# Sliding-window attention and a multiplicative feed-forward on one core: gates on GpSimd, parted up products, half loads and a last tile in column halves

## The chip, the cores and the metric

The kernel runs on one NeuronCore of a Trainium2 chip. The metric is the device time of one execution in microseconds (us). A core has TensorE (PE, matrix products into PSUM), VectorE (DVE), ScalarE (ACT), GpSimd (POOL) and SyncE (SP), each with a queue of its own that it works off in order, and 16 DMA engines. PSUM has eight banks; each matrix product of this kernel is written to one bank, a group of scores to four and a value step to two.

## The reference

```python
# q, k, v: (8 batches, 8 heads, 576 rows, 64); heads 0-3: plain window of 32; heads 4-7: 32 rows at a distance of 4
scores = q @ k.T / 8;  scores = where(mask[h], scores, -1e9)
attn = exp(scores - max) / (sum + 1e-9)
x = (attn @ v) as (4608 tokens, 512)
out = ((x @ w1) * (x @ w2)) @ w3 @ w_out        # 512 -> 1024 -> 1024 -> 512, float32 out
```

## The kernel before

**Data flow.** q, k and v come in row form. VectorE transposes 32 x 32 blocks (`turn`, lines 379 and 394) so that the head dimension lies on partitions. The queries stand in an order by residue modulo 4, so that the dilated window is a plain window of 32 in each residue class. A half batch `u` (0: plain heads, 1: dilated heads) has six blocks `m` of 96 queries against 128 keys. `Group.scores` (line 445) writes scores of up to five blocks over four banks; `exps` (line 456, ScalarE) takes the exponential into a tile `et`; in later batches `masks` (line 464, VectorE) multiplies by a 0/1 mask, which GpSimd makes once in `masks_of_bias` (line 358), while batch 0 has a bias added by matmuls (line 428). A `Step` covers three blocks of one half: `values` (line 481) multiplies by v with a column of ones, `recip` and `norm` (lines 492, 504, VectorE) divide, and `back` and `keep` (lines 521, 529) transpose on TensorE and copy into XT in the first two batches; later batches use a DMA transpose. So each batch has four steps, 0 to 3. Batch 0 and 1 bring v through transposes on TensorE (`v_back`, line 403) and copies (`v_keep`, lines 413 and 415).

**The feed-forward** works in 16 units of 288 tokens. For a unit k and an f of eight 128-column slices, `up` (line 553) makes A(k,f) with w1 and B(k,f) with w2, each four matmuls over the four 128-row chunks of x, in the order 2, 3, 0, 1. Chunks 0 and 1 come from the plain heads (steps 0 and 1 of the batch), chunks 2 and 3 from the dilated heads (step 2 for an even unit, step 3 for an odd one). `copy_a` (line 564) takes A to SBUF as bf16 on ScalarE; `gate` (line 569) multiplies it by B, straight from PSUM, on VectorE, into `gt`. `down` (line 580) multiplies a tile of 128 tokens by the fused weight, 8 matmuls of 512 columns; `copy_y` (line 591) takes it to SBUF and `store` writes it out. The fused weight wf = w3 @ w_out is made once: `w3_back` (line 622) transposes a slice of w3, `w3_keep` (line 629) copies it on ScalarE, `w3_mul` (line 634) multiplies, and `w3_done` (lines 645, 647) keeps the result. `finish` (lines 601, 602) ends the last tile.

**The planner.** Every piece of work is a task with an engine, a duration in ns, the tasks that it needs and a priority; the smaller number goes first. `Plan.run` plays them through in time: a free engine takes the ready task of best priority, and the order of starts is the order in which instructions are written to each engine's queue. The queue "DMA" of the plan is GpSimd: loads are issued from it, and identity, bias and masks are computed on it. A load occupies it for its issue time alone:

```python
if e == "DMA":
    free[e] = now + t.dur[0]
    if t.dur[1]:
        dma = max(dma, now + t.dur[0]) + t.dur[1]
        t.end = dma + 1900
```

Loads get a rising priority number in the order in which they are named: four for batch 0, then those of `FIRST_LOADS` ("w0" are two loads, columns of w1 and w2; "30" is slice 0 of w3; "o0" half of w_out; "q1" the q of batch 1), then those of later batches. The masks have 26.5, the gates -1. `RANK` and `FIRST` hold priorities of the kinds of attention work: T a transpose on VectorE, S scores, E exponential, VT and VK the two parts of bringing v, V values, N the division, X and K the way back into XT, W and C the w3 transposes and their copies. `ON_DVE` names the copies that VectorE does instead of ScalarE. As long as TensorE has nothing and the first up product has not begun, the plan adds fillers (`fill`, line 676); `warm_up` (line 659) stands at the beginning.

Of the kernel before, what the change touches and what calls it, by code (L numbers as in the profile page):

```python
# [19 lines left out]
S = 576  # L20
# [6 lines left out]
UNIT = 288  # L27
RING = 1152
BIG = 30000.0
BIASED = 1  # L30
LATE = False
TURNED = 2
DIRECT_V = 2
ORDER = (2, 3, 0, 1)
RES = (0, 2, 1, 3)
RANK = dict(E=0.4, VK=2, K=0.3, N=1.5, T=3, VT=0.3, S=0.4, V=0.05, X=0.2, W=6, C=-1)
FIRST = {"E": 2, "VK": 0.4, "K": 0.5, "N": 0.2, "T": 2, "VT": 0.05, "S": 0.2, "V": 0.05, "X": 0.4}
WARM = 14
FILL = 110
FIRST_LOADS = ("30", "31", "w0", "w1", "32", "w2", "o0", "o1", "q1", "k1", "33", "34", "v1", "35", "36", "37")  # L40
SHIFT = {}
ON_DVE = ("VK0.0.1", "VK1.0.1", "W3D1", "W3D3", "W3D7")
GRP = 5
WHOLE = ("qn", "kn")
BUSY = 4500
LEAD = 1.1


class Task:
# [10 lines left out]
class Plan:  # L60
# [119 lines left out]
def kernel(  # L180
# [46 lines left out]
    kts = [const.tile([P, 2, PADK + S, 2], BF16, name=f"kt{i}") for i in range(2)]  # L227
    qts = [const.tile([P, 2, S, 2], BF16, name=f"qt{i}") for i in range(2)]
    vts = [const.tile([P, 2, PADK + S, 2], BF16, name=f"vt{i}") for i in range(1)]
    warm = const.tile([P, 512], BF16, name="warm")  # L230

    def bank(n, dtype=F32):
        at = ps[:, plan.now.place or 0, :]
        return (at if dtype == F32 else at.bitcast(dtype))[:, 0:n]
# [79 lines left out]
    w3n, w3T = {}, {}  # L314
# [226 lines left out]
    held = {}  # L541
# [5 lines left out]
            return XT[0][:, b * BLK : (b + 1) * BLK, c, 48 * hf : 48 * hf + 48]  # L547
        return XT[1][:, k, c - 2, :].rearrange("p (r m t) -> p m r t", r=2, m=BLK)

    def up(k, f, w_sb, key):  # L550
        o = bank(UNIT)
        for j, c in enumerate(ORDER):
            nc.tensor.matmul(  # L553
                out=o,
                lhsT=w_sb[:, c, f * P : (f + 1) * P],
                rhs=unit_cols(k, c),
                start=(j == 0),
                stop=(j == DCH - 1),
            )
        held[(key, k, f)] = o  # L560

    def copy_a(k, f):
        a_sb = wk_pool.tile([P, UNIT], BF16, tag="asb", bufs=6, name="asb")
        nc.scalar.copy(out=a_sb, in_=held[("a", k, f)])  # L564
        held[("s", k, f)] = a_sb

    def gate(k, f):
        c0 = (k * UNIT) % RING
        nc.vector.tensor_tensor(  # L569
            out=gt[:, f, c0 : c0 + UNIT].rearrange("p (r m t) -> p m r t", r=2, m=BLK),  # L570
            in0=held[("b", k, f)].rearrange("p (m r t) -> p m r t", r=2, m=BLK),
            in1=held[("s", k, f)].rearrange("p (m r t) -> p m r t", r=2, m=BLK),
            op=AL.mult,
        )

    def down(i):
        y = bank(d_model)
        c0 = (i * P) % RING
        for f in range(KFF):
            nc.tensor.matmul(  # L580
                out=y,
                lhsT=gt[:, f, c0 : c0 + P],
                rhs=wf_sb[:, f, :],
                start=(f == 0),
                stop=(f == KFF - 1),
            )
        held[("y", i)] = y
# [3 lines left out]
        nc.scalar.copy(out=o_sb, in_=held[("y", i)])  # L591
        held[("o", i)] = o_sb

    def finish(i):

        o_sb = wk_pool.tile([P, d_model], F32, tag="osb", bufs=3, name="osb")
        b, x = i * P // S, i * P % S
        row = b * S + 4 * (x % RUN) + RES[x // RUN]
        rows = out[row : row + 4 * (P - 1) + 1 : 4, :]
        lo, hi = slice(0, d_model // 2), slice(d_model // 2, d_model)  # L600
        nc.scalar.copy(out=o_sb[:, lo], in_=held[("y", i)][:, lo])
        nc.vector.tensor_copy(out=o_sb[:, hi], in_=held[("y", i)][:, hi])
        nc.scalar.dma_start(out=rows[:, lo], in_=o_sb[:, lo])
        nc.sync.dma_start(out=rows[:, hi], in_=o_sb[:, hi])

    def store(i):
        o_sb = held[("o", i)]
# [17 lines left out]
        held[("x3", ft)] = x  # L625

    def w3_keep(ft):
        w3T[ft] = wk_pool.tile([P, KFF, P], BF16, tag="w3T", bufs=3, name="w3T")
        nc.scalar.copy(out=w3T[ft], in_=held[("x3", ft)])  # L629

    def w3_mul(ft):
# [22 lines left out]
        return (RANK if b else FIRST)[kind]  # L654

    def warm_up():
        o = bank(512)
        for i in range(WARM):
            nc.tensor.matmul(out=o, lhsT=warm[:, 0:P], rhs=warm, start=True, stop=True)

# [12 lines left out]
            nc.vector.memset(t[0:32, :, 0, 0:D], 0.0)  # L673

    def fill():
        nc.tensor.matmul(out=bank(256), lhsT=warm[:, 0:P], rhs=warm[:, 0:256], start=True, stop=True)  # L676
# [18 lines left out]
    def loads_rows(nm, b, us=None):  # L695
        old = turned.get((nm, b - 2), [])
        for u in (0, 1) if us is None else us:
            L[(nm, b, u)] = None
        sl = slice(0, 2) if us is None else slice(us[0], us[-1] + 1)
        t = load(f"L{nm}{b}", 700, 3100 if us is None else 1600, old,  # L700
                 lambda: load_rows(nm, rows_of[nm], b, sl))
        for u in (0, 1) if us is None else us:
            L[(nm, b, u)] = t
# [26 lines left out]
    for u in range(2):  # L730
        for nm in ("qn", "kn", "vn"):
            if u or nm not in WHOLE:
                loads_rows(nm, 0, (u,))
# [6 lines left out]
    for x in FIRST_LOADS:  # L740
        c = int(x[1])
        if x[0] == "w":
            lw12[c] = loads_w12(c)
        elif x[0] == "o":
            lwo[c] = load(f"LWO{c}", 600, 3300, [], lambda c=c: load_wo(c))
        elif x[0] == "3":
            lw3[c] = load(f"LW3.{c}", 550, 1400, [], lambda ft=c: load_w3(ft))
        elif x[0] == "v" and DIRECT_V <= c:
            loads_v(c)
        else:  # L750
            loads_rows(x[0] + "n", c)

    FUSED, w3m = [], []
    for ft in sorted(lw3):
        x = add(f"W3T{ft}", "PE", 450, [lw3[ft], idt], lambda f=ft: w3_back(f), RANK["W"], slot=1,
                after=w3m[-3:-2])
        y = add("W3C", "ACT", 1012, [x], lambda f=ft: w3_keep(f), RANK["C"], lat=100, after=w3m[-3:-2])
        if ft + 7 in lw3:
            lw3[ft + 7].after.append(x)
            lw3[ft + 7].deps.append(x)  # L760
        z = add(f"W3M{ft}", "PE", 1728, [y, lwo[0], lwo[1]], lambda f=ft: w3_mul(f), 7, slot=1)
        w3m.append(z)
        name = f"W3D{ft}"
        eng, dur = ("DVE", 688) if name in ON_DVE else ("ACT", 585)
        FUSED.append(add(name, eng, dur, [z], lambda f=ft, e=eng: w3_done(f, e), -1, lat=100))
# [138 lines left out]
            prev["x"][i] = x  # L904
            vdone.setdefault(bb, []).append(vv)

    seq = 10
    G, Y, gates, stores, pairs = {}, {}, [], [], []

    def ups(k, f):  # L910
        nonlocal seq
        b, hf = k // 2, k % 2
        need = kept[b][0:2] + kept[b][2 + hf : 3 + hf]
        wl = lw12[(0, 0, 1, 1, 2, 2, 2, 2)[f]]
        lap = k * UNIT - RING
        free = [Y[i] for i in range(max(0, lap // P), (lap + UNIT - 1) // P + 1)]
        seq += 1
        a = add(f"A{k}.{f}", "PE", 490, need + wl, lambda: up(k, f, w1_sb, "a"), seq, slot=1,
                after=free + pairs[-1:])
        pairs.append(a)  # L920
        ca = add("CA", "ACT", 400, [a], lambda: copy_a(k, f), -1, lat=100,
                 after=[gates[-6] if len(gates) > 5 else None])
        seq += 1
        bb = add(f"B{k}.{f}", "PE", 490, need + wl, lambda: up(k, f, w2_sb, "b"), seq,
                 slot=1, after=[a])
        G[(k, f)] = add("G", "DVE", 460, [bb, ca], lambda: gate(k, f), -1, lat=100)
        gates.append(G[(k, f)])

    def downs(i):
        nonlocal seq  # L930
        seq += 1
        ks = {i * P // UNIT, (i * P + P - 1) // UNIT}
        y = add(f"Y{i}", "PE", 1728, [G[(k, f)] for k in ks for f in range(KFF)] + FUSED,
                lambda: down(i), seq, slot=1)
        Y[i] = y
        if i == n_y - 1:
            add("FIN", "ACT", 400, [y], lambda: finish(i), -1, lat=100, after=stores[-3:-2])
            return
# [58 lines left out]
```

## Time and profile before

| | |
|---|---|
| median of 3 runs | 256.36 us (256.32 to 256.38) |
| profiled execution, own time | 256.45 us |
| its span | 254.7 us |
| granted TensorE clock | 0.999 |
| first up product on TensorE | 21.6 us |
| first fused-weight product | 36.0 us |
| last matmul ends | 250.4 us |
| 128 gates on VectorE (line 569) | 57.7 us, 455 ns each |
| 128 copies of A on ScalarE (line 564) | 50.8 us, 398 ns each |
| five mask instructions on GpSimd (line 358) | 4.76 us together |

The time is that of the whole execution; the span is from the first instruction to the last, and 1.75 us lie around it. In timelines the columns are start in us, length in us, engine, line, operation with output and inputs, count, and in brackets the idle time before it with what ended it.

### The profile page before, as it was taken

To read this page: it belongs to the slowest core of one execution; us is meant where nothing else is said; L and a number is where in the kernel's file an instruction comes from. 1 tells how busy PE (TensorE), PEld (TensorE's weight loads), DVE (VectorE), ACT (ScalarE), POOL (GpSimd) and SP (SyncE) were. 2 spreads that over 40 slices of the span, in tenths; PEclk is the share of its full clock that TensorE was granted. 3 is DMA by queue.
4 is the path that set the end of the run, shared out by engine and by line. 5 is a ranking of instruction groups with operands and counts; after the bars stand their busy time and mean duration, and the time that the engine had idled before them with its cause. 6 is when DMAs were issued, how large, how long until landed. Compare 5 with 4: busy or idle time off the path is not lost.

```text
span 254.7 us, 6758 instructions
## 1 busy us (share of the span) xinstructions
PE 244.5 (96%) x2723; PEld 169.2 (66%) x2755; DVE 165.4 (65%) x341; ACT 126.0 (49%) x221; POOL 66.3 (26%) x103
## 2 busy tenths in 40 slices
PE   7699999999999999999999999999999999999993
PEld 3488766565767666667676766676767667777661
DVE  3983447799889888678767877837737365333220
ACT  5677333986635534462626526355353543333331
POOL 7653129543522712008260310700000000000000
PEclk9999999999999999999999999999999999999999
DMA  7999999999999999828999967952232223311113
GB/s 224 210 198 206 205 212 210 208 100 190 188 136 168 210 181 181 190 66 143 165 118 136 141 76 103 133 88 64 66 65 67 66 68 67 106 41 44 41 41 124
DMA packets 59230, 33.40 MB, mean 131 GB/s; under 512 B 44736, under 2 KB 49088, under 8 KB 59200
## 3 DMA queue, kind: packets, MB, share of 16 engines
q0 software_dynamic: 38544, 18.81, 58.6%
q1 hardware_dynamic: 20512, 14.03, 23.4%
q8 instruction: 21, 0.34, 0.6%
q10 hardware_dynamic: 144, 0.13, 0.2%
q14 instruction: 9, 0.07, 0.1%
HBM read 38.80 MB, written 9.44 MB: 189 GB/s over the span
## 4 chain that ended last, share of the span: by engine, by line
PE 92%; ACT 3%; DMA 2%; DVE 1%; issue 1%; ACTq 0%
PE ps L553 50%; PE ps L580 24%; PE ps L634 5%; PE ps L481 4%; PE ps L445 4%; DMA gt<-in_q_dram 2%; ACT et L456 2%; PE ps L676 2%; PE ps L622 1%; PE ps L403 1%; PE ps L521 1%; ACT w3T L629 1%; DVE qt L394 1%; ACT qn L271 0%; DVE kt L379 0%
## 5 line engine op out<-in xcount | busy, mean ns | idle before, releaser
L553 PE MATMUL ps<-XT,w_sb 128*128 128x288 bf16 x1024 | 136.2, 286 | 0.0
L553 PEld LDWEIGHTS <-w_sb 128*128 128x128 bf16 x1024 | 97.8, 98 | 30.6
L569 DVE TENSOR_TENSOR gt<-ps,asb 128x288 bf16<-128x288 f32 x128 | 57.7, 455 | 51.9 <-PE ps L553 49.6
L564 ACT CAST asb<-ps 128x288 bf16<-128x288 f32 x128 | 50.8, 398 | 51.9 <-PE ps L553 49.6
L580 PE MATMUL ps<-wf_sb,gt 128*128 128x512 bf16 x260 | 65.9, 379 | 1.5
L591 ACT COPY osb<-ps 128x512 f32<-128x512 f32 x35 | 20.5, 585 | 56.4 <-PE ps L580 54.6
L580 PEld LDWEIGHTS <-gt 128*128 128x128 bf16 x288 | 28.2, 98 | 27.8
L293 POOL DMA_DIRECT2D vp<-in_v_dram x48 | 29.9, 629 | 40.1 <-PE ps L481 20.8
L456 ACT ACTIVATE et<-ps 128x1920 bf16<-128x1920 f32 (+2 forms) x21 | 34.2, 1633 | 5.6 <-PE ps L445 4.8
L504 DVE TENSOR_TENSOR xo<-ps,rcp 96x384 bf16<-96x384 f32 (+1 forms) x48 | 31.5, 676 | 0.6
L464 DVE TENSOR_TENSOR et<-et,mask 128x960 bf16<-128x960 bf16 (+1 forms) x34 | 21.4, 646 | 4.9 <-ACT et L456 4.7
L394 DVE STREAM_TRANSPOSE qt<-qn 128x320 uint32<-128x320 uint32 (+3 forms) x34 | 22.4, 669 | 2.1 <-ACT qn L271 1.9
L481 PEld LDWEIGHTS <-et 128*128 128x128 bf16 x384 | 14.3, 98 | 1.7
L481 PE MATMUL ps<-vp,et 128*128 128x65 bf16 x384 | 15.1, 193 | 0.0
L634 PE MATMUL ps<-wo_sb,w3T 128*128 128x512 bf16 x60 | 14.4, 379 | 0.4
L394 DVE STREAM_TRANSPOSE kt<-kn 128x320 uint32<-128x320 uint32 (+3 forms) x18 | 11.6, 645 | 4.4 <-PE ps L445 4.3
L445 PE MATMUL ps<-qt,kt 32*128 32x96 bf16 x768 | 12.1, 201 | 1.9 <-DVE kt L379 1.9
L445 PEld LDWEIGHTS <-kt 32*128 32x128 bf16 x768 | 9.1, 92 | 7.0 <-issue 4.5
L492 DVE RECIPROCAL rcp<-ps 96x12 f32<-96x12 f32 x32 | 6.8, 216 | 10.5 <-PE ps L481 10.2
L245 POOL DMA_DIRECT2D kn<-in_k_dram x8 | 5.5, 685 | 29.0 <-DVE kt L394 16.7
L379 DVE STREAM_TRANSPOSE kt<-kn 128x576 uint32<-128x576 uint32 (+1 forms) x9 | 9.9, 1118 | 1.4 <-PE ps L445 1.4
L634 PEld LDWEIGHTS <-w3T 128*128 128x128 bf16 x64 | 5.9, 98 | 6.8 <-ACT w3T L629 0.6
(53 smaller groups left out, 114.6 us busy)
## 6 DMA issues: line engine op xcount, KB each, us to landing
qn<-in_q_dram POOLq DMA_DIRECT2D x7, 576.0 KB, 8.3
kn<-in_k_dram POOLq DMA_DIRECT2D x7, 576.0 KB, 7.5
w3n<-in_moe_w_dram POOLq DMA_DIRECT2D x8, 256.0 KB, 15.1
out_dram<-osb SPq DMA_DIRECT2D x7, 256.0 KB, 2.6
out_dram<-osb SPq DMA_DIRECT2D x8, 224.0 KB, 2.9
vp<-in_v_dram POOLq DMA_DIRECT2D x6, 288.0 KB, 10.4
out_dram<-osb SPq DMA_DIRECT2D x8, 192.0 KB, 2.7
out_dram<-osb SPq DMA_DIRECT2D x8, 160.0 KB, 3.9
```

What stands on the lines that cost most here:

```text
L293: nc.gpsimd.dma_start(out=vp[32 + p0 : 32 + p0 + n, 4:8, m, 0:D], in_=v_rows(b, 4, 4 * t0 + res, [[4 * D, n], [S * D, 4], [1, D]]),)
L394: nc.vector.transpose(out=o, in_=i)
L445: nc.tensor.matmul(out=self.sp[:, g, QB * i : QB * i + QB], lhsT=kt[prt, u, QB * m : QB * m + P, c], rhs=qq, start=(c == 0 and not biased) ...
L456: nc.scalar.activation(out=ev, in_=self.sp[:, :, 0:x], func=ACT.Exp, scale=scale)
L464: nc.vector.tensor_tensor(out=ev, in0=ev, in1=mk, op=AL.mult)
L481: nc.tensor.matmul(out=self.o[:, g, mm, :], lhsT=grp.et[:, c0 : c0 + P], rhs=vps[self.b % 2][:, 4 * self.u + g, 3 * self.hf + mm, 0 : D + ...
L504: nc.vector.tensor_tensor(out=dst, in0=self.o[0:QB, hs, :, 0:D], in1=self.rcp[0:QB, hs, :].unsqueeze(3).to_broadcast([QB, n, 3, D]), op=AL ...
L553: nc.tensor.matmul(out=o, lhsT=w_sb[:, c, f * P : (f + 1) * P], rhs=unit_cols(k, c), start=(j == 0), stop=(j == DCH - 1),)
L564: nc.scalar.copy(out=a_sb, in_=held[("a", k, f)])
L569: nc.vector.tensor_tensor(out=gt[:, f, c0 : c0 + UNIT].rearrange("p (r m t) -> p m r t", r=2, m=BLK), in0=held[("b", k, f)].rearrange("p ( ...
L580: nc.tensor.matmul(out=y, lhsT=gt[:, f, c0 : c0 + P], rhs=wf_sb[:, f, :], start=(f == 0), stop=(f == KFF - 1),)
L634: nc.tensor.matmul(out=o, lhsT=w3T[ft][:, g, :], rhs=wo_sb[:, g, :], start=(g == 0), stop=(g == KFF - 1),)
```

## The change

- `LATE` is set: the scores of batch 0's last step and the last v transposes wait for the values of step 2. Priorities, `LEAD` and the up products' first number differ. Warm-up is 24 matmuls of 256 columns instead of 14 of 512.
- Batch 1's loads come by halves ("k10" is k of batch 1, half 0), and in another order among the weights. `B0_LOADS` writes out batch 0's loads, in the order that they had.
- Twelve copies instead of five are on VectorE, K0.2 among them.
- Eighteen gates of units 0, 1 and 2 go to GpSimd: ScalarE first copies B to SBUF as float32 (`copy_b`), and GpSimd multiplies. There are two buffers for these copies.
- The first four up products are cut in two tasks: chunks 0 and 1, which need steps 0 and 1 alone, and then chunks 2 and 3.
- There are two buffers w3T instead of three.
- The last tile is made in two halves of 256 columns. VectorE copies the first, and 128 columns of the second; ScalarE copies the rest.

```diff
-LATE = False
+LATE = True
-RANK = dict(E=0.4, VK=2, K=0.3, N=1.5, T=3, VT=0.3, S=0.4, V=0.05, X=0.2, W=6, C=-1)
-FIRST = {"E": 2, "VK": 0.4, "K": 0.5, "N": 0.2, "T": 2, "VT": 0.05, "S": 0.2, "V": 0.05, "X": 0.4}
-WARM = 14
+RANK = dict(E=0.3, VK=0.2, K=1.5, N=0.4, T=0.2, VT=0.1, S=0.05, V=0.05, X=0.2, W=6, C=2)
+FIRST = {"E": 0.5, "VK": 2, "K": 0.5, "N": 1, "T": 1.5, "VT": 0.3, "S": 0.1, "V": 0.2, "X": 0.4}
+WARM = 24
-FIRST_LOADS = ("30", "31", "w0", "w1", "32", "w2", "o0", "o1", "q1", "k1", "33", "34", "v1", "35", "36", "37")
+FIRST_LOADS = ("w0", "30", "w1", "31", "k10", "w2", "o0", "o1", "32", "33", "q10", "v10", "v11", "34", "35", "36", "q11", "k11", "37")
-ON_DVE = ("VK0.0.1", "VK1.0.1", "W3D1", "W3D3", "W3D7")
+ON_DVE = ("K0.2", "K1.1", "K1.2", "VK0.0.0", "VK0.0.1", "VK0.1.1", "VK1.0.0", "W3D0", "W3D2", "W3D4", "W3D5", "W3D6")
+B0_LOADS = ("v0", "q1", "k1", "v1")
+ON_POOL = ("G0.0", "G0.2", "G0.3", "G0.4", "G0.6", "G0.7", "G1.0", "G1.1", "G1.2", "G1.4", "G1.6", "G1.7", "G2.1", "G2.2", "G2.3", "G2.4", "G2.5", "G2.6")
+PARTED = 4
-LEAD = 1.1
+LEAD = 1.2
...
+    def copy_b(k, f):
+        b_sb = wk_pool.tile([P, UNIT], F32, tag="bsb", bufs=2, name="bsb")
+        nc.scalar.copy(out=b_sb, in_=held[("b", k, f)])
+        held[("b", k, f)] = b_sb
+
-    def gate(k, f):
+    def gate(k, f, eng):
         c0 = (k * UNIT) % RING
-        nc.vector.tensor_tensor(
+        (nc.gpsimd if eng == "DMA" else nc.vector).tensor_tensor(
...
+    def finish(i, half):
...
+        c0, n = half * d_model // 2, d_model // 2 if half == 0 else d_model // 4
+        nc.vector.tensor_copy(out=o_sb[:, c0 : c0 + n], in_=held[("y", i, half)][:, 0:n])
+        nc.sync.dma_start(out=rows[:, c0 : c0 + n], in_=o_sb[:, c0 : c0 + n])
+        if half == 1:
+            nc.scalar.copy(out=o_sb[:, c0 + n :], in_=held[("y", i, half)][:, n:])
+            nc.scalar.dma_start(out=rows[:, c0 + n :], in_=o_sb[:, c0 + n :])
...
-        w3T[ft] = wk_pool.tile([P, KFF, P], BF16, tag="w3T", bufs=3, name="w3T")
+        w3T[ft] = wk_pool.tile([P, KFF, P], BF16, tag="w3T", bufs=2, name="w3T")
...
-    seq = 10
+    seq, parted = 20, 0
...
+        def product(key, after):
+            nonlocal seq, parted
+            name = f"{key.upper()}{k}.{f}"
+            seq += 1
+            if k or parted == PARTED:
+                return add(name, "PE", 490, need + wl, lambda: up(k, f, key), seq, slot=1,
+                           after=after), []
+            parted += 1
+            p = add(name + "p", "PE", 245, need[0:2] + wl,
+                    lambda: up(k, f, key, ORDER[2:], last=False), seq - 5, slot=1, after=after)
+            return add(name, "PE", 245, need + [p],
+                       lambda: up(k, f, key, ORDER[:2], first=False), seq), [p]
...
+        if f"G{k}.{f}" in ON_POOL:
+            bb = add("CB", "ACT", 420, bb, lambda: copy_b(k, f), -1, lat=100,
+                     after=[pooled[-2] if len(pooled) > 1 else None])
+            G[(k, f)] = add("G", "DMA", (900, 0), [bb, ca], lambda: gate(k, f, "DMA"), -1, lat=150)
+            pooled.append(G[(k, f)])
+        else:
+            G[(k, f)] = add("G", "DVE", 460, bb + [ca], lambda: gate(k, f, "DVE"), -1, lat=100)
```

More of the change, by code (lines that the diff above doesn't have):

```diff
@@ L229 @@
     vts = [const.tile([P, 2, PADK + S, 2], BF16, name=f"vt{i}") for i in range(1)]
-    warm = const.tile([P, 512], BF16, name="warm")
+    warm = const.tile([P, 256], BF16, name="warm")
     def bank(n, dtype=F32):
@@ L548, in unit_cols, with up @@
         return XT[1][:, k, c - 2, :].rearrange("p (r m t) -> p m r t", r=2, m=BLK)
-    def up(k, f, w_sb, key):
-        o = bank(UNIT)
-        for j, c in enumerate(ORDER):
+    def up(k, f, key, chunks=ORDER, first=True, last=True):
+        if first:
+            held[(key, k, f)] = bank(UNIT)
+        for j, c in enumerate(chunks):
             nc.tensor.matmul(
-                out=o,
-                lhsT=w_sb[:, c, f * P : (f + 1) * P],
+                out=held[(key, k, f)],
+                lhsT={"a": w1_sb, "b": w2_sb}[key][:, c, f * P : (f + 1) * P],
                 rhs=unit_cols(k, c),
-                start=(j == 0),
-                stop=(j == DCH - 1),
+                start=(first and j == 0),
+                stop=(last and j == len(chunks) - 1),
             )
-        held[(key, k, f)] = o
     def copy_a(k, f):
@@ L592, in copy_y, with down_part @@
         held[("o", i)] = o_sb
-    def finish(i):
-        o_sb = wk_pool.tile([P, d_model], F32, tag="osb", bufs=3, name="osb")
+    def down_part(i, half):
+        y = bank(d_model // 2)
+        c0 = (i * P) % RING
+        for f in range(KFF):
+            nc.tensor.matmul(
+                out=y,
+                lhsT=gt[:, f, c0 : c0 + P],
+                rhs=wf_sb[:, f, half * d_model // 2 : (half + 1) * d_model // 2],
+                start=(f == 0),
+                stop=(f == KFF - 1),
+            )
+        held[("y", i, half)] = y
+    def finish(i, half):
+        if half == 0:
+            held[("o", i)] = wk_pool.tile([P, d_model], F32, tag="osb", bufs=3, name="osb")
+        o_sb = held[("o", i)]
         b, x = i * P // S, i * P % S
@@ L599, in finish @@
         rows = out[row : row + 4 * (P - 1) + 1 : 4, :]
[L600 to L604, printed above, removed]
+        c0, n = half * d_model // 2, d_model // 2 if half == 0 else d_model // 4
[4 more added lines that the diff above has]
+            nc.scalar.dma_start(out=rows[:, c0 + n :], in_=o_sb[:, c0 + n :])
     def store(i):
@@ L656, in warm_up @@
     def warm_up():
-        o = bank(512)
+        o = bank(256)
         for i in range(WARM):
@@ L675, in fill @@
     def fill():
-        nc.tensor.matmul(out=bank(256), lhsT=warm[:, 0:P], rhs=warm[:, 0:256], start=True, stop=True)
+        nc.tensor.matmul(out=bank(256), lhsT=warm[:, 0:P], rhs=warm, start=True, stop=True)
     plan.fill, plan.fill_from = fill, 2000
@@ L681 @@
     c0 = add("const2", "DVE", 1400, [c1], constants, -98)
-    add("warm", "PE", 700 + 427 * WARM, [c1], warm_up, 0)
+    add("warm", "PE", 700 + 213 * WARM, [c1], warm_up, 0)
     lw3, lwo = {}, {}
@@ L729 @@
     plan.dma = 1200 + 1350 * len(WHOLE)
[L730 to L733, printed above, removed]
+    for x in B0_LOADS:
+        loads_rows(x[0] + "n", 0, (int(x[1]),))
     idt = add("ident", "DMA", (600, 0), [], lambda: make_identity(nc, ident), 2.5, lat=150)
@@ L750 @@
         else:
-            loads_rows(x[0] + "n", c)
+            loads_rows(x[0] + "n", c, (int(x[2]),) if x[2:] else None)
     FUSED, w3m = [], []
@@ L755 @@
         x = add(f"W3T{ft}", "PE", 450, [lw3[ft], idt], lambda f=ft: w3_back(f), RANK["W"], slot=1,
-                after=w3m[-3:-2])
-        y = add("W3C", "ACT", 1012, [x], lambda f=ft: w3_keep(f), RANK["C"], lat=100, after=w3m[-3:-2])
+                after=w3m[-2:-1])
+        y = add("W3C", "ACT", 1012, [x], lambda f=ft: w3_keep(f), RANK["C"], lat=100, after=w3m[-2:-1])
         if ft + 7 in lw3:
@@ L905 @@
             vdone.setdefault(bb, []).append(vv)
-    seq = 10
-    G, Y, gates, stores, pairs = {}, {}, [], [], []
+    seq, parted = 20, 0
+    G, Y, gates, stores, pairs, pooled = {}, {}, [], [], [], []
     def ups(k, f):
@@ L916, in ups @@
         free = [Y[i] for i in range(max(0, lap // P), (lap + UNIT - 1) // P + 1)]
-        seq += 1
-        a = add(f"A{k}.{f}", "PE", 490, need + wl, lambda: up(k, f, w1_sb, "a"), seq, slot=1,
-                after=free + pairs[-1:])
+        def product(key, after):
[10 more added lines that the diff above has]
+                       lambda: up(k, f, key, ORDER[:2], first=False), seq), [p]
+        a, p = product("a", free + pairs[-1:])
         pairs.append(a)
-        ca = add("CA", "ACT", 400, [a], lambda: copy_a(k, f), -1, lat=100,
+        ca = add("CA", "ACT", 400, [a] + p, lambda: copy_a(k, f), -1, lat=100,
                  after=[gates[-6] if len(gates) > 5 else None])
[L923 to L926, printed above, removed]
+        bb, p = product("b", p or [a])
+        bb = [bb] + p
+        if f"G{k}.{f}" in ON_POOL:
[5 more added lines that the diff above has]
+            G[(k, f)] = add("G", "DVE", 460, bb + [ca], lambda: gate(k, f, "DVE"), -1, lat=100)
         gates.append(G[(k, f)])
@@ L932, in downs @@
         ks = {i * P // UNIT, (i * P + P - 1) // UNIT}
-        y = add(f"Y{i}", "PE", 1728, [G[(k, f)] for k in ks for f in range(KFF)] + FUSED,
-                lambda: down(i), seq, slot=1)
+        need = [G[(k, f)] for k in ks for f in range(KFF)] + FUSED
+        if i == n_y - 1:
+            for half in range(2):
+                y = add(f"Y{i}{'ab'[half]}", "PE", 880, need, lambda h=half: down_part(i, h),
+                        seq + half, slot=1)
+                add("FIN", "DVE", 300, [y], lambda h=half: finish(i, h), half, lat=100,
+                    after=stores[-3:-2])
+            return
+        y = add(f"Y{i}", "PE", 1728, need, lambda: down(i), seq, slot=1)
         Y[i] = y
-        if i == n_y - 1:
-            add("FIN", "ACT", 400, [y], lambda: finish(i), -1, lat=100, after=stores[-3:-2])
-            return
         cy = add("CY", "ACT", 585, [y], lambda: copy_y(i), -1, lat=100,
```

## The prediction

> **What bounds the kernel now.** I read the page first, then TensorE's timeline, the GpSimd timeline beside the DMA issues, and the end of the timeline. The page says that TensorE is busy nearly always:
>
> ```profile
> PE 244.5 (96%) x2723; PEld 169.2 (66%) x2755; DVE 165.4 (65%) x341; ACT 126.0 (49%) x221; POOL 66.3 (26%) x103
> ```
>
> I turn this into a ledger with paces from the chain of waits: 1024 up matmuls at 122.5 ns (100 took 12.25 us), 288 down and 64 fused-weight matmuls at 216.5 ns (8 took 1.73), 768 scores at 13.75, 384 values at 30.4, 64 w3 and 48 v transposes at 56, 48 back transposes at 43, 16 bias matmuls at 122. That is 125.4 + 76.2 + 10.6 + 11.7 + 3.6 + 2.7 + 2.1 + 2.0 = 234.3 us of useful work. The last down matmul ends at 250.4, so 16.1 us are idle or filler. Some 7.8 us of useful work lie before the first up product at 21.77, so 14.0 of the 16.1 are lost there and 2.1 later. TensorE's timeline shows the loss at its best place:
>
> ```profile
> 16.19 1.80 PE L676 MATMUL ps<-warm 128*128 128x256 bf16 x15
> ...
> 19.39 1.80 PE L676 MATMUL ps<-warm 128*128 128x256 bf16 x15
> ...
> 21.61 1.63 PE L553 MATMUL ps<-XT,w_sb 128*128 128x288 bf16 x12
> ```
>
> The 30 fillers are 3.3 us of waiting for the third copy into XT (K0.2). In ScalarE's timeline that copy is queued behind an exponential and a value copy:
>
> ```profile
> 18.90 1.13 ACT L456 ACTIVATE et<-ps 128x1152 bf16<-128x1152 f32 x1 [0.78 <-PE ps L445]
> 19.93 0.79 ACT L413 COPY vp<-ps 128x768 bf16<-128x768 bf16 x1
> 20.61 0.66 ACT L529 COPY XT<-ps 128x576 bf16<-128x576 bf16 x1
> ```
>
> From 22 on TensorE has work at almost every moment (busy 21.95 of 22.00 us in the stretch 22:44). Whatever moves the start of this stretch moves the end.
>
> The second reading is GpSimd's queue, since gates will stand in it:
>
> ```profile
> 9.40 0.74 POOL L303 DMA_DIRECT2D w_sb<-in_moe_w_dram  x1 [0.73 <-DMA qn<-in_q_dram]
> 10.79 0.54 POOL L318 DMA_DIRECT2D w3n<-in_moe_w_dram  x1 [0.64 <-DMA kn<-in_k_dram]
> ...
> 31.97 0.53 POOL L318 DMA_DIRECT2D w3n<-in_moe_w_dram  x1 [2.22 <-PE ps L553]
> 35.48 0.70 POOL L245 DMA_DIRECT2D qn<-in_q_dram  x1 [2.98 <-ACT asb L564]
> 37.85 0.71 POOL L245 DMA_DIRECT2D kn<-in_k_dram  x1 [1.67 <-DVE qt L394]
> 38.58 4.76 POOL L358 TENSOR_SCALAR mask<-bias 128x384 bf16<-128x384 bf16 x5
> ```
>
> and the DMA issue that answers the fourth of these lines, with its time to landing last:
>
> ```profile
> qn<-in_q_dram POOLq DMA_DIRECT2D x1, 576.0 KB, 17.2
> ```
>
> That load, the sixteenth on GpSimd, was issued at 17.73 and landed at 34.9; the twenty-fourth is issued at 35.48. The pattern holds for all that I matched: load 9 leaves at 7.92 (load 1 landed at 7.64), 10 at 9.40 (9.1), 11 at 10.79 (10.5), 12 at 12.14 (11.9), 25 at 37.85 (37.3), 33 at 52.64 (52.35). **A load waits for the landing of the one eight before it, and GpSimd stands still meanwhile.** The named releasers "PE" and "ACT" had long been done. The masks show what that means for computing there: their input was ready at about 4 us, yet they ran at 38.58, directly behind the twenty-fifth load. The planner that writes the queue knows no limit of eight. It issues loads back to back at 0.55 to 0.8 us, so in its own time the masks stood at 18.5 us.
>
> **What the Trainium skill says.** "GPSIMD Engine Reference", section 3.1, gives about 2.6 cycles an element at 1.2 GHz for a two-input operation: 288 elements are an estimated 0.62 us and a start-up. No gate on GpSimd is in the trace; its one-input rows of 288 took 937 ns. I take 0.85. "SBUF — State Buffer", Who interferes with whom, says that a VectorE instruction with at most one SBUF input, outside the 2-port modes, does not contend with GpSimd: gates left on VectorE read PSUM and one SBUF tile. Nothing here shows it. "TensorE: Matmul & The Clock Gate", part 1, says that an idle window of about 3.4 us halves the clock, and about 3.4 us of work restores it. The first seven warm-up matmuls at 423 ns (1.54 to 4.50), then about 216, agree with the second half; an idle of that length is not in the trace.
>
> **The change, part by part.**
>
> The head loses real waits. K0.2 goes to VectorE (0.46) and no longer stands behind the two instructions above; the fused-weight copies (2 x 0.97 on ScalarE at 15.1) yield to K0.0 and K0.1. From N0.2's end at 17.7: 0.3 for its transpose, 0.46 for the copy, 0.1 of handing on, so unit 0 can start at about 18.5 instead of 21.77. VectorE takes two more value copies (2 x 0.95), so the fourth step comes at about 23.1 against 24.2. Until then unit 0 gives 8 products (3.9 us) where the kernel before had done 3 by 23.3: 5 x 0.49 = 2.45 us. The four halved products only reorder 16 matmuls; at most they take 1 us of filler's place, which is inside that figure if K0.1 is late. w0 one place earlier and w1 likewise land at about 14.5 and 18.3, early enough; w2 lands at 26, as before.
>
> The tail: now 256 columns on ScalarE, then 256 on VectorE:
>
> ```profile
> 250.50 0.37 ACT L601 COPY osb<-ps 128x256 f32<-128x256 f32 x1 [1.14 <-PE ps L580]
> ...
> 250.91 0.42 DVE L602 COPY osb<-ps 128x256 f32<-128x256 f32 x1 [5.10 <-ACT osb L601]
> ```
>
> After, only the second half's two 128-column copies follow the last matmul. From the pairs 256/512 (372/585 and 425/684 ns) they cost about 0.29 + 0.27, again in turn: 0.83 becomes 0.56, a gain of 0.27. The matmuls are 16 x 0.109 (the fillers' pace) instead of 8 x 0.216: nothing.
>
> Costed at nothing: W3D and K on other engines (0.69 against 0.585 and 0.46 against 0.66, hidden by TensorE's queue; without that cover, under 1 us), two w3T buffers for three (a 1.02 copy beside a 1.73 product), LEAD, ranks of later batches, warm-up length (TensorE waits for k at 8.84 either way).
>
> The gates: 18 times, 0.42 more on ScalarE (the row of 0.398, float output) and 0.455 less on VectorE; neither is full between 22 and 44 (8.98 and 12.21 us of 22). **Their place in GpSimd's queue is the cost.** In the planner's time all loads without a condition are issued by 18.3: 4.2 for the first four and the constants, then 14.05 for w0 to k11. Gate G0.0 needs K0.2, then B0.0, its copy and 0.2 of handing on, 20 to 22 in the planner's time. So it is written behind load 25 (k11); behind load 26 ("37", which waits for the first w3 transpose); behind the masks, which fill the planner's 18.8 to 21.3; and perhaps behind load 27. On the chip I estimate landings from the old ones (288 KB 1.4, 256 KB 1.27, 512 KB 2.5 us, load 4 at 11.9): w0b 14.4, 30 15.7, w1b 18.3, 31 19.6, k10 21.0, w2b 26, o1 31, "32" 32.3, "33" 33.5, q10 34.9. Load 25 leaves after load 17 landed: 33.8 + 0.7. Load 26 after load 18: 35.2 + 0.55 = 35.8. Masks 4.76: 40.5. Load 27, 0.7: 41.2. G0.0 ends at about 42.
>
> Who waits: the fp32 copies have two buffers, so the third (for B0.3, due at about 23.5) waits for G0.0, and ScalarE with it. Behind it in order are the bf16 copies of a, perhaps K0.3, and all fused-weight copies. TensorE can put some 5 more products into the eight PSUM banks, to about 26, and then stands. It resumes at about 42.5, after gate and copy. Done by then: batch 0's attention 7.15 (1.3 + 2.0 + 1.4 + 1.5 + 1.0), 13 products 6.4, two w3 transposes 0.9: 14.4. Left: 219.9. Add 1.5 for a cold clock (half of the 3 us above; 0 if it stays warm, 1.7 at most) and 1.3 of later stalls (before 2.1; the loads then lie ready). The last matmul ends at 42.5 + 219.9 + 1.5 + 1.3 = 265.2 against 250.4: +14.8, less 0.27. The profiled execution, 256.45 with 254.7 of span, becomes 271.0; the median of 256.36 stands 0.09 lower: **270.9**.
>
> Both ends of the unknown terms: G0.0 ends at 37 if the masks come after it, at 34 if also the last two loads do; at 44 if a second load stands ahead. Five products more or fewer are 2.5. A GpSimd gate of 0.7 to 1.2 moves it by under 1 in front, but twelve of them with ten load issues between (10.2 + 6.7 us) nearly fill the 15.7 us of 32 products, so up to 4 us more if loads of batch 2 hold gates up again.
>
> **The rivals.** *Short stall*: the gates stand before masks and the last loads. G0.0 ends at 34 to 37: 5 to 8 us less, 262.5 to 266. Against it: the masks have been ready since 4 us and GpSimd is free in the plan before any gate. *No stall, faster*: one mechanism, the place of G0.0. If GpSimd finishes it by about 26 us, ScalarE's third copy and the eight banks hide all, and the head's 2.45 and the tail's 0.27 remain: 253.6. For it: VectorE and ScalarE are light there, and GpSimd computes only 26% of the span. Against it: that idle time is blocked time. *The edits don't bite*: if K0.1 or the fourth step sets unit 1's start as before, and nothing stalls, it is 256.1. *GpSimd becomes the bound over units 0 to 2*: the long stall and 4 to 6 more, 275 to 277.
>
> **How the numbers follow.** Long stall, with or without the last rival: 0.71, its own range 265 to 277. Short stall: 0.12. Faster: 0.15. Within 0.2% (0.5 us, about what a measurement of this kernel can tell from no change): 0.02. So slower 0.83. From 258 to 278 both stalls are held with some room for a better overlap, and about 0.8; the faster case is left out.
>
> **What would show it.** Right: the first gate on GpSimd starts after 39 us, behind the five mask instructions; ScalarE's fp32 copy waits for it over 10 us; TensorE is idle from about 26 to 42, then runs without gaps; slow matmuls for 3 us after 42. The tail's two last copies are 0.3 us each. Wrong: a gate on GpSimd before 26 us, up products at 18.5 without an interruption, and an end near 252.

## The result and the profile after

The kernel after takes **276.21 us** (six runs, 275.77 to 276.39) against 256.37 for the kernel before beside it (256.32 to 256.64): 1.077 times as long, with a 95% interval of 1.0755 to 1.0783, or 19.8 us more. The profiled execution took 276.18 us with a span of 274.1 and a mean granted clock of 0.969.

The page after, its engine totals and three rows of its 40 slices (6.85 us each):

```profile
PE 248.7 (91%) x2782; PEld 173.2 (63%) x2782; DVE 162.4 (59%) x331; ACT 129.0 (47%) x232; POOL 81.3 (30%) x124
...
PE   7799003999999999999999999999999999999994
...
POOL 8542279940313678300825121340000000000000
PEclk9999855899999999999999999999999999999999
```

TensorE has one hole, two slices of 0 and one of 3, then 9 to the end. The clock is low in and just after the hole and nowhere else. In these three slices GpSimd shows 2, 7 and 9 (the issuing of loads counts as busy here): at first it mostly stands, then it works. So nearly the whole loss is one event, and GpSimd's timeline at that place shows it:

```profile
36.58 0.53 POOL L321 DMA_DIRECT2D w3n<-in_moe_w_dram  x1 [1.10 <-DMA qn<-in_q_dram]
37.14 4.75 POOL L361 TENSOR_SCALAR mask<-bias 128x384 bf16<-128x384 bf16 x5
41.85 0.75 POOL L248 DMA_DIRECT2D qn<-in_q_dram  x1
42.59 0.73 POOL L248 DMA_DIRECT2D kn<-in_k_dram  x1
43.31 1.22 POOL L282 DMA_DIRECT2D vp<-in_v_dram  x1
44.52 0.76 POOL L577 TENSOR_TENSOR gt<-bsb,asb 128x288 bf16<-128x288 f32 x1
```

Line 577 is the gate. The first one, G0.0, starts at 44.52, behind the last load of w3, the five masks and three load issues of batch 2. ScalarE's timeline shows who waits (line 567 copies A, line 572 copies B to float32):

```profile
24.90 0.65 ACT L532 COPY XT<-ps 128x576 bf16<-128x576 bf16 x1
25.43 0.42 ACT L567 CAST asb<-ps 128x288 bf16<-128x288 f32 x1
45.31 0.40 ACT L572 COPY bsb<-ps 128x288 f32<-128x288 f32 x1 [19.47 <-POOL gt L577]
```

The third float32 copy needs a buffer that only a gate frees, and it stands at the head of ScalarE's queue for 19.47 us. TensorE's timeline (line 557 is `up`, four matmuls to a product):

```profile
20.65 1.14 PE L557 MATMUL ps<-XT,w_sb 128*128 128x288 bf16 x8
...
22.44 2.12 PE L557 MATMUL ps<-XT,w_sb 128*128 128x288 bf16 x16
...
24.66 2.62 PE L557 MATMUL ps<-XT,w_sb 128*128 128x288 bf16 x20
45.76 11.38 PE L557 MATMUL ps<-XT,w_sb 128*128 128x288 bf16 x76 [18.49 <-ACT bsb L572]
```

TensorE fills its banks by 27.3 and stands for 18.49 us. The kernel before ran on at that place:

```profile
23.79 12.41 PE L553 MATMUL ps<-XT,w_sb 128*128 128x288 bf16 x100
```

After the stall TensorE of the kernel after shows no idle time: busy 20.00 of 20.00 us in the stretch 60:80, 40.00 of 40.00 in each stretch of 40 from there to 240. The end of the timeline, with the two copies of the last half tile (lines 624 and 627):

```profile
270.40 0.29 DVE L624 COPY osb<-ps 128x128 f32<-128x128 f32 x1 [0.45 <-PE ps L606]
...
270.77 0.27 ACT L627 COPY osb<-ps 128x128 f32<-128x128 f32 x1 [1.49 <-DVE osb L624]
```

The last matmul ends at about 270.4, against 250.4 before.

### The profile page after: what moved, and what is told of

Its sections match the earlier page's. It is cut to its first block, busy times and chain, and to the rows that moved or that the text cites. A ratio compares the mean times of both kernels' runs of the same rounds, so it can differ in the third digit from the quotient of the medians.

```text
span 274.1 us, 6851 instructions
## 1 busy us (share of the span) xinstructions
PE 248.7 (91%) x2782; PEld 173.2 (63%) x2782; DVE 162.4 (59%) x331; ACT 129.0 (47%) x232; POOL 81.3 (30%) x124
## 4 chain that ended last, share of the span: by engine, by line
PE 82%; DMA 12%; POOL 3%; issue 1%; ACT 0%; DVE 0%; POOLq 0%; ACTq 0%
PE ps L557 45%; PE ps L588 22%; DMA qn<-in_q_dram 8%; PE ps L658 5%; DMA w3n<-in_moe_w_dram 4%; PE ps L484 4%; PE ps L448 3%; POOL mask L361 1%; PE ps L646 1%; PE ps L606 1%; PE ps L406 0%; POOL vp L282 0%; PE ps L524 0%; POOL gt L577 0%; POOL qn L248 0%
## 5 line engine op out<-in xcount | busy, mean ns | idle before, releaser
L557 PE MATMUL ps<-XT,w_sb 128*128 128x288 bf16 x1024 | 137.4, 289 | 18.5 <-ACT bsb L572 18.5
L577 DVE TENSOR_TENSOR gt<-ps,asb 128x288 bf16<-128x288 f32 x110 | 49.7, 455 | 78.4 <-PE ps L557 52.6
L588 PEld LDWEIGHTS <-gt 128*128 128x128 bf16 x280 | 27.1, 98 | 27.3
L296 POOL DMA_DIRECT2D vp<-in_v_dram x48 | 30.9, 654 | 28.6 <-PE ps L484 18.6
L577 POOL TENSOR_TENSOR gt<-bsb,asb 128x288 bf16<-128x288 f32 x18 | 13.3, 750 | 14.8 <-ACT bsb L572 14.7
L572 ACT COPY bsb<-ps 128x288 f32<-128x288 f32 x18 | 7.2, 401 | 22.0 <-POOL gt L577 20.5
L658 PE MATMUL ps<-wo_sb,w3T 128*128 128x512 bf16 x64 | 15.0, 379 | 0.0
L653 ACT COPY w3T<-ps 128x1024 bf16<-128x1024 bf16 x8 | 8.1, 1017 | 4.9 <-PE ps L646 4.9
```

What stands on the lines that cost most here:

```text
L296: nc.gpsimd.dma_start(out=vp[32 + p0 : 32 + p0 + n, 4:8, m, 0:D], in_=v_rows(b, 4, 4 * t0 + res, [[4 * D, n], [S * D, 4], [1, D]]),)
L557: nc.tensor.matmul(out=held[(key, k, f)], lhsT={"a": w1_sb, "b": w2_sb}[key][:, c, f * P : (f + 1) * P], rhs=unit_cols(k, c), start=(first ...
L577: (nc.gpsimd if eng == "DMA" else nc.vector).tensor_tensor(out=gt[:, f, c0 : c0 + UNIT].rearrange("p (r m t) -> p m r t", r=2, m=BLK), in0 ...
L588: nc.tensor.matmul(out=y, lhsT=gt[:, f, c0 : c0 + P], rhs=wf_sb[:, f, :], start=(f == 0), stop=(f == KFF - 1),)
L658: nc.tensor.matmul(out=o, lhsT=w3T[ft][:, g, :], rhs=wo_sb[:, g, :], start=(g == 0), stop=(g == KFF - 1),)
```

## The experiments

**Theory.** GpSimd's order was written by a plan that knows nothing of the wait of each load for the landing of the one eight before it. The first gates are therefore queued behind late loads and the masks; ScalarE's queue and then TensorE stop until GpSimd arrives. **Rivals.** Computing on GpSimd is itself too slow (the gates become the bound); the other edits (priorities, halves, parts, copies on VectorE) cost time; the masks alone are the delay.

### No gate on GpSimd (e1_no_pool)

```diff
-ON_POOL = ("G0.0", "G0.2", ..., "G2.6")
+ON_POOL = ()
```

> The changed kernel with all 128 gates on VectorE again; everything else of the change stays. Theory (the gates' place in GpSimd's queue is the whole loss): TensorE has no idle stretch between 27 and 46 us, and what is left is a head and a tail that are each about 0.3 us better: 255.8 us, 255.2 to 256.6. Rival (the other edits cost too: two w3T buffers, seven more copies on VectorE, half loads): over 258. Rival (the head's full forecast gain of 2.45 us appears once the stall is gone): 253.6.

Measured: 259.36 us, 1.0117 of before (1.0099 to 1.0135). The long stall is gone and 16.9 of the 19.8 us with it; TensorE's longest pause at that place is now 0.73 us:

```profile
26.43 9.96 PE L557 MATMUL ps<-XT,w_sb 128*128 128x288 bf16 x80 [0.73 <-ACT XT L532]
```

But 3.0 us of loss remain, over the range expected: in this order the other edits are not free. The largest remaining wait is seen in ScalarE's timeline and in the DMA issues between 58 and 66 us (columns: size, then us from issue to landing):

```profile
69.65 0.58 ACT L599 COPY osb<-ps 128x512 f32<-128x512 f32 x1 [2.86 <-DMA out_dram<-osb]
```
```profile
out_dram<-osb SPq DMA_DIRECT2D x1, 256.0 KB, 8.9
```

The copy of an output tile waits for its buffer, whose store took 8.9 us to land; before, the corresponding store took 5.7. An exponential queued behind that copy is late, and TensorE is busy 17.95 of 20 us between 60 and 80 (before 19.79).

### The first two gates alone, and two late ones (x3_first_two, x4_late_two)

```diff
-ON_POOL = ("G0.0", "G0.2", ..., "G2.6")
+ON_POOL = ("G0.0", "G0.2")      # x3_first_two
+ON_POOL = ("G0.6", "G0.7")      # x4_late_two
```

> The changed kernel with only G0.0 and G0.2 on GpSimd, in the same place of its queue, so that two fp32 buffers suffice. Theory (a late gate costs through the first buffer that runs out): ScalarE is now held by the bf16 copies, of which there are six; the seventh (pair 6, A1.2) waits for G0.0. TensorE goes on to about 31.6 us and then stands until about 45.5: 271 us, 269 to 273. Rival (it is only the pair of fp32 buffers): no stall, 256. Rival (the late gate itself, whatever the buffers): as long a stall as in the changed kernel, 275 to 276.

> The changed kernel with only G0.6 and G0.7 on GpSimd: two fp32 buffers suffice, and the bf16 buffers of these pairs are needed again only in unit 2, after 57 us. Theory (a gate that is late but holds no buffer that is wanted costs nothing): the gates run after 50 us and the time is that of the kernel with none on GpSimd, 255.2 to 256.8. Rival (any gate behind those loads costs): 262 or more.

Measured: 270.46 (1.0558, 1.0532 to 1.0585) and 258.24 (1.008, 1.0064 to 1.0095). Two early gates cost 11.1 us more than none; two late ones cost nothing beside e1's level. With two gates the float32 buffers suffice, so another copy blocks. The first fence is ScalarE's timeline, the second TensorE's:

```profile
45.03 0.70 ACT L567 CAST asb<-ps 128x288 bf16<-128x288 f32 x2 [12.55 <-POOL gt L577]
```
```profile
24.53 9.97 PE L557 MATMUL ps<-XT,w_sb 128*128 128x288 bf16 x80
45.48 4.00 PE L557 MATMUL ps<-XT,w_sb 128*128 128x288 bf16 x16 [10.98 <-ACT asb L567]
```

Where five products ran without a pause in the kernel after, twenty now do before TensorE stops at 34.5, and the wait is 10.98 us: the buffers ahead of the late gate set how long TensorE goes on, and the gate sets when it resumes. How long was not foreseen: the stop was expected at 31.6, at the seventh bf16 copy, since there are six buffers, and it came at the twelfth. Why, no view shows. The 16 matmuls after the stop took 3.8 us instead of 2.0, so the cold clock cost 1.8 here. In x4_late_two the late gates run at this place of GpSimd's timeline:

```profile
55.40 1.43 POOL L577 TENSOR_TENSOR gt<-bsb,asb 128x288 bf16<-128x288 f32 x2
```

Unit 0's A and B have long been ready by then, yet no engine waits for these gates: what is late must also be needed. Its time missed the number expected, because that assumed no loss from the other edits.

### A plan that knows the wait (e2_plan8)

```diff
+                        if e == "DMA" and t.dur[1] and len(lands) >= 8 and lands[-8] > now:
+                            continue
...
                             t.end = dma + 1900
+                            lands.extend([t.end] * (2 if t.dur[0] == 1200 else 1))
...
-            ahead = [f for f in free.values() if f > now]
+            ahead = [f for f in free.values() if f > now] + [x for x in lands if x > now]
```

> The changed kernel with all eighteen gates on GpSimd, but the planner holds a load back until the load eight before it has landed, so that gates and masks are written between the loads. Theory (order in the queue, not the engine, is the loss): the first gate on GpSimd starts before 25 us, no stall, 254 to 257 us. Rival (GpSimd is too slow for these gates, or the way through an fp32 copy is itself the cost): a stall or slower units 0 to 2 remain, over 262 us.

Measured: 256.03, 0.9982 of before (0.9974 to 0.9991), as expected, with the same 18 gates and the same durations in the plan. GpSimd's timeline and TensorE's (line numbers are three higher):

```profile
23.54 0.73 POOL L580 TENSOR_TENSOR gt<-bsb,asb 128x288 bf16<-128x288 f32 x1 [0.81 <-ACT bsb L575]
```
```profile
24.52 11.93 PE L560 MATMUL ps<-XT,w_sb 128*128 128x288 bf16 x96
```

The first gate runs at 23.54 instead of 44.52, and TensorE makes 24 products without a pause where it had stopped after five. GpSimd makes the same gates and masks and is busy as long as in the kernel after (81.4 against 81.3 us): its speed is not the bound. This decides for the order and against the rival. The new plan also writes the other engines' queues in another order; that the first gate's place is what counts there, the next experiment shows, which shortens GpSimd's queue alone.

### The masks on VectorE (e5_masks_dve)

```diff
-            nc.gpsimd.tensor_scalar(   # in masks_of_bias
+            nc.vector.tensor_scalar(
```

> The changed kernel with its five mask instructions on VectorE instead of GpSimd; no other instruction changes its place. GpSimd's queue ahead of the first gate is shorter by 4.75 us, but load 27 may not leave before 36.6, load 29 not before 39.3. Theory (the place of the first gate sets the length of the stall, one for one): the first gate starts at 40.8 instead of 44.5 us, the stall is 3.7 us shorter: 272.5 us, 271.5 to 273.5. Rival (the stall is set by something else, the landing of batch 1's data for example): 276.

Measured: 273.59 (1.0656, 1.0638 to 1.0673), 2.6 us less than the kernel after, just over the range expected. GpSimd's timeline, then TensorE's:

```profile
40.28 1.20 POOL L282 DMA_DIRECT2D vp<-in_v_dram  x1 [0.32 <-DMA w3n<-in_moe_w_dram]
41.49 0.74 POOL L577 TENSOR_TENSOR gt<-bsb,asb 128x288 bf16<-128x288 f32 x1
```
```profile
42.72 11.55 PE L557 MATMUL ps<-XT,w_sb 128*128 128x288 bf16 x76 [15.28 <-ACT bsb L572]
```

Taking 4.75 us of masks away brings the gate forward by 3.03 only, because the loads behind them now wait for landings themselves. The stall shrinks by 3.2 and the time by 2.6. The time follows the first gate nearly one for one, and the masks are a part of the delay, not the delay.

### The gates alone, in the kernel before (e4_gates_only)

The kernel before, with the 18 gates, `copy_b`, the plan's two branches for them, and what makes room for the buffers (two w3T, 24 warm-up matmuls of 256 columns). Priorities, loads and copies are as before.

```diff
+        if f"G{k}.{f}" in ON_POOL:
+            bb = add("CB", "ACT", 420, [bb], lambda: copy_b(k, f), -1, lat=100, ...)
+            G[(k, f)] = add("G", "DMA", (900, 0), [bb, ca], lambda: gate(k, f, "DMA"), -1, lat=150)
```

> The kernel before with the eighteen gates on GpSimd and no other part of the change, but for what makes room: two w3T buffers and the shorter warm-up tile. Theory (the gates alone make the loss, in any order of the head): GpSimd reaches the first gate after load 25, the masks and the first loads of v, at about 45 us; the third fp32 copy holds ScalarE, and TensorE stands for some 16 to 19 us: 275 us, 272 to 278. Rival (the loss needs the changed order of loads and priorities): under 266.

Measured: 281.72 (1.0969, 1.0937 to 1.1), 5.5 us over the kernel after and 3.7 over the range expected. GpSimd's timeline, then TensorE's:

```profile
44.99 0.74 POOL L575 TENSOR_TENSOR gt<-bsb,asb 128x288 bf16<-128x288 f32 x1
```
```profile
46.22 11.78 PE L554 MATMUL ps<-XT,w_sb 128*128 128x288 bf16 x72 [17.16 <-ACT bsb L570]
```

The gates alone are enough for the stall. The ups begin later, at 23.25, but that is not what is added: 11 products are done before the stall as in the kernel after, and TensorE resumes only 0.5 us later. Most of the 5.5 us comes after that. TensorE is idle for 1.9 us between 66.6 and 69.2, and 15 fused-weight matmuls at a fallen clock then take 4.9 us where 3.2 is the pace; another 1.9 us are idle between 75 and 240, where the kernel after has none; and the tail is the old one. The clock also fell once before the stall. Two rows of the busy table by stretches (columns: stretch, its length, busy time of PE, PEld, DVE, ACT, POOL with counts, granted clock, DMA share, GB/s):

```profile
10.00:15.00 5.00, 4.74 (x89) 3.58 (x88) 3.84 (x11) 2.92 (x4) 2.48 (x4) 0.66 1.21 204
...
68.00:72.00 4.00, 3.49 (x47) 1.65 (x48) 2.39 (x3) 2.84 (x3) 0.00 (x0) 0.63 1.11 213
```

### The tail alone, and the plan's limit with it, in the kernel before (e6_tail, e8_before_plan8_tail)

```diff
-    def finish(i):
+    def finish(i, half):
...
-            add("FIN", "ACT", 400, [y], lambda: finish(i), -1, lat=100, after=stores[-3:-2])
+            for half in range(2):
+                y = add(f"Y{i}{'ab'[half]}", "PE", 880, need, lambda h=half: down_part(i, h), ...)
+                add("FIN", "DVE", 300, [y], lambda h=half: finish(i, h), half, lat=100, ...)
```

The second kernel adds to this the three edits of e2_plan8.

> The kernel before with the last tile in column halves alone. Theory: the two copies after the last matmul take 0.56 instead of 0.83 us: 256.1 us, a ratio of 0.9990 (0.9984 to 0.9996). Rival (the last store's landing or its issue sets the end, so nothing is gained): 1.000.

> The kernel before, all gates on VectorE, with the planner that holds a load back until the load eight before it has landed, and the last tile in column halves. Only the masks then stand earlier on GpSimd. Theory (the limit matters to computing on GpSimd alone, and nothing waits there in the kernel before): the tail's gain and no more, 256.1 us, 255.6 to 256.6. Rival (the planner's order improves everywhere): below 255.5. Rival (loads held up behind the masks delay the weights): over 257.

Measured: the tail 255.81 (0.9976, 0.9967 to 0.9985), so 0.6 us won, twice what was expected. The end of its timeline:

```profile
250.37 0.29 DVE L616 COPY osb<-ps 128x128 f32<-128x128 f32 x1 [0.45 <-PE ps L598]
...
250.74 0.27 ACT L619 COPY osb<-ps 128x128 f32<-128x128 f32 x1 [1.49 <-DVE osb L616]
...
251.04 0.37 ACTq L620 DMA_DIRECT2D out_dram<-osb  x1
```

The last store leaves at 251.04 instead of 251.36, and with 64 KB it lands in 1.8 us where 128 KB took 2.1. The second 0.3 was left out of the prediction.

With the plan's limit added it is 257.78 (1.0067, 1.0041 to 1.0093): the expectation, the tail's gain and no more, fell. The number is that of the rival *loads held up behind the masks delay the weights*, but not its cause: the up products begin at 21.31, no later than before. The new order has a pause of 1.27 us in front of a score group that waits for an exponential, and 18.73 busy us of 20 between 60 and 80. The likely reading is that priorities belong to the plan for which they were chosen; it was not isolated further.

### A fourth output buffer on top of e1 (e9_osb4)

```diff
-        o_sb = wk_pool.tile([P, d_model], F32, tag="osb", bufs=3, name="osb")
+        o_sb = wk_pool.tile([P, d_model], F32, tag="osb", bufs=4, name="osb")
...
-                    after=stores[-3:-2])
+                    after=stores[-4:-3])
```

> The changed kernel with no gate on GpSimd (259.4 us) and four instead of three buffers for output tiles. In that kernel's trace four down products come within 9 us at 58 us, while loads fill the DMA engines; a store then lands after 8.9 us, and ScalarE waits 2.9 us for its buffer. Theory (this wait is most of what the other edits cost): 257.4 us, 256.6 to 258.2. Rival (the order of the work around it costs, not the buffer): 259 or more.

Measured: 258.49 (1.0073, 1.0058 to 1.0088), 0.9 us less than e1 and not the 2 expected. The buffer wait is gone (20.00 of 20 busy between 60 and 80), but 2.1 us over before remain: TensorE is busy 21.27 of 22 between 22 and 44 (before 21.95) and 38.28 of 40 between 80 and 120 (before 39.68). The waits named there are for the fourth step's copy K0.3 (0.73), for an exponential (1.13) and for a DMA transpose (0.51). They point to the changed order of the work; which of the edits makes them was not settled.

### Value copies back on ScalarE, and without parts (e10_head, e11_unparted)

```diff
-ON_DVE = ("K0.2", "K1.1", "K1.2", "VK0.0.0", "VK0.0.1", "VK0.1.1", "VK1.0.0", ...)
+ON_DVE = ("K0.2", "K1.1", "K1.2", "VK0.0.1", "VK1.0.0", ...)      # e10_head: e2_plan8 with this
...
-PARTED = 4
+PARTED = 0                                                        # e11_unparted: e10_head with this
```

> The changed kernel with the planner that knows the limit of eight (256.03 us), and two of the value copies of batch 0, VK0.0.0 and VK0.1.1, back on ScalarE. Theory (the head gained little because these two copies, 0.95 us each on VectorE, stand ahead of the last division, so that unit 1 starts no earlier than in the kernel before): K0.3 comes about 1 us earlier and with it the end: 255.2 us, 254.6 to 255.8. Rival (the transposes of k, behind K0.2 on VectorE, or ScalarE with more to do set it): 256.0 or more.

> The kernel of 255.50 us (planner that knows the limit, two value copies back on ScalarE) with the first up products whole instead of in two parts. There the third copy into XT (K0.2) ends at 19.0 us and the second (K0.1) at 17.1, and the parts let four to eight matmuls start at 18.3. Theory (the parts fill time in which TensorE waits for K0.2, but K0.3 then sets unit 1's start): little is lost, 0 to 0.5 us: 255.7 us, 255.4 to 256.2. Rival (the parts are what made the head shorter): 256.3 or more.

Measured: 255.50 (0.9961, 0.9949 to 0.9973) and 255.66 (0.9957, 0.994 to 0.9974). TensorE's timeline of e10_head:

```profile
18.28 0.66 PE L560 MATMUL ps<-XT,w_sb 128*128 128x288 bf16 x4
...
24.87 5.30 PE L560 MATMUL ps<-XT,w_sb 128*128 128x288 bf16 x42 [1.01 <-ACT XT L535]
```

The first up matmuls now start at 18.28, 2.2 us before e2_plan8's. Yet only 0.5 us is won: TensorE runs out of work at the fourth step, whose copy K0.3 starts at 24.15 instead of 24.76 and ends a pause of 1.01 us. The gain is about what K0.3 came earlier by (0.6). With whole products instead of parts the ratio is the same, so the parts are worth nothing that can be measured. Of the kernels run, e10_head has the lowest median, below both kernels, but e11_unparted and e6_tail are not clearly behind it.

### The plan with measured loads, masks and gates (e7_plan8_measured)

```diff
-            load("LW", 800, (1700, 1700, 3300)[c], ...)       # and the other loads likewise
+            load("LW", 800, (1270, 1270, 2500)[c], ...)
...
-    mk = add("masks", "DMA", (2500, 0), [blk], masks_of_bias, 26.5, lat=150)
+    mk = add("masks", "DMA", (4750, 0), [blk], masks_of_bias, 26.5, lat=150)
...
-            G[(k, f)] = add("G", "DMA", (900, 0), ...)
+            G[(k, f)] = add("G", "DMA", (700, 0), ...)
```

> The changed kernel with the planner that knows the limit of eight, and with the planner's loads at the measured spacing (256 KB 1270 ns, 288 KB 1400, 512 KB 2500, 576 KB 2850), masks at 4750 and a GpSimd gate at 700. Theory (with the queue's order right the rest is bound by TensorE, so better landing times change little): 255.5 us, 254.5 to 256.5. Rival (the priorities were fitted to the old durations and scatter): 257 or more.

Measured: 261.0 (1.0176, 1.015 to 1.0202), where 255.5 was expected. It is slower than e2_plan8 by 5 us, with several pauses (TensorE busy 20.15 of 22 between 22 and 44, 17.25 of 20 between 60 and 80). No single one explains it. Truer durations under the same priorities made a worse order, as in e8_before_plan8_tail.

## Why the prediction was right, and where it was off

**Direction, mechanism and place were right.** The first gate stands behind the masks (forecast: after 39 us; measured 44.52). The third float32 copy waits over 10 us (19.47). TensorE is idle from about 26 to 42.5 (27.3 to 45.76), then runs without gaps, with slow matmuls first. e2_plan8 shows that the cause is the order, since the same gates in another order cost nothing; e5_masks_dve that the first gate's place in GpSimd's queue sets the length of the stall; and e4_gates_only that the gates suffice for it. The measured 276.2 also lies in the range of the rival *GpSimd becomes the bound over units 0 to 2* (275 to 277), but that is chance: TensorE waits for no gate after 46 us. Two readings behind that rival were loose. Its 10.2 + 6.7 = 16.9 us do not nearly fill 15.7 us, they exceed it. And the 26% of the span on GpSimd are mostly the issuing of loads; its computing was about 6.4 of the 66.3 us.

**The time was 5.3 us too low** (270.9 against 276.2), and the terms of the sum show where:

| step | forecast | measured | effect, us |
|---|---|---|---|
| TensorE resumes | 42.5 | 45.76 | +3.3 |
| products done before the stall | 13 | 11 | +1.0 |
| cold clock | 1.5 | 1.9 | +0.4 |
| later stalls | 1.3 | 1.8, as a remainder | +0.5 |

*The queue place* failed in the step "perhaps behind load 27". Three loads stand ahead of G0.0, not one: q and k of batch 2 and the first of v, 2.7 us of issues together, on masks that began at 37.14 where the forecast's 35.8 was too early by 1.3. The forecast had priced a second load as its upper end (44) and that was nearer. The queue shows that order; why the plan chose it over mine was not traced.

*The head* failed in the step "unit 0 can start at about 18.5". K0.2 did move (it ends on VectorE at 18.66), but then K0.1 was last, ending on ScalarE at 19.75; VectorE had divided for the third step before the second. A score group and v transposes went ahead of the products too, so the ups began at 20.65. The fourth step's copy K0.3 ended at 25.55 and not at about 23.1, later than in the kernel before (24.2). With 11 products done at the stall, the head was worth little; this was the rival *the edits don't bite*, whose 256.1 lies beside the 256.03 of e2_plan8, where nothing stalls. There is luck in that closeness: the tail was worth 0.6, not 0.27, so that head, gates and the other edits together gained nothing in e2_plan8. That they cost some 0.2 is not clear of the noise.

*The cold clock*: the first 76 up matmuls after the stall took 11.22 us where 9.31 is the pace. The Trainium skill, "TensorE: Matmul & The Clock Gate", part 1, makes it an estimated 1.7 (half speed for 3.4 us). The run shows a little more: the granted clock was 0.50 from 45.8 to 49.2 us and 0.75 in the microsecond after.

*The later stalls* are only the remainder of the sum. The trace shows no idle time after 46 us, so nothing in it says where this time lies.

*Costed at nothing* was wrong, but hidden: without the gates these edits cost 3.0 us, 3.6 against the tail alone (e1_no_pool, e6_tail). An output buffer that comes late is 0.9 of it (e9_osb4). The sentence on cover named only engine durations; it left out that a changed order puts more stores among the loads, and what waits for their buffers. That points to the order and not to the edits by themselves: e2_plan8 has them all and does not pay. In the kernel after the cost does not show either: no store leaves there between 55 and 75 us, and between 60 and 80 the DMA engines move 59 GB/s where they moved 181 before. Its stores from 80 to 130 us do land late (6.5 us in the median), yet TensorE is never idle there; why not was not settled.

*The gate itself* was well priced. Two rows of the groups of the kernel after (columns: busy us and mean ns; then idle time before, and what ended most of it):

```profile
L577 POOL TENSOR_TENSOR gt<-bsb,asb 128x288 bf16<-128x288 f32 x18 | 13.3, 750 | 14.8 <-ACT bsb L572 14.7
L572 ACT COPY bsb<-ps 128x288 f32<-128x288 f32 x18 | 7.2, 401 | 22.0 <-POOL gt L577 20.5 <-PE ps L557 0.2
```

750 ns lies between the 620 estimated from the Trainium skill, "GPSIMD Engine Reference", section 3.1, which leave out the start-up, and the 850 taken. Both rows name each other as releaser. Read alone this looks like two slow engines; the count and the mean say that neither is.

## What to carry to other kernels

Before work is put on an engine that also issues loads, look at how long its issues wait in the trace, and put the work where that queue really is, not where a plan without those waits has it. A late instruction costs only from the point where the buffers in front of it run out: count buffers and banks, add their work to the time of the last free one, and compare with the time of the late instruction. That count is rough: in x3_first_two the stop came five copies later than counted. When a plan or its durations are corrected, measure again: the same priorities may then give a worse order, as two runs here did.

## What was not expected of the hardware

- In e4_gates_only the granted clock fell to 0.66 after TensorE had been idle for 2.11 us (7.0 to 9.1), and to 0.63 after idle stretches of 1.67 and 0.20 us. The Trainium skill, "TensorE: Matmul & The Clock Gate", part 1, names an idle window of about 3.4 us; this run shows a fall after less. The kernel before was idle for 1.86 us at the first of these places and kept 1.00, but its warm-up is another one, so that the idle time may not be the whole reason.
- A two-input gate on GpSimd with 288 elements took 750 ns, less than the one-input mask rows of the same width (924 ns in the kernel after, 937 before).
- In e1_no_pool a store of 256 KB took 8.9 us while the DMA engines moved some 200 GB/s; such stores took 3.9 us in the median of that run and 2.8 in the kernel after.
